# V in 4 MB transfers of all heads, P turned by VectorE, and other wo parts, in a decode kernel on one core

## The chip, the core and the metric

The kernel runs on one NeuronCore of a Trainium2 chip. TensorE (PE) multiplies, VectorE (DVE) and ScalarE (ACT) work elementwise and move PSUM to SBUF, GpSimd (POOL) prepares constants, and SyncE (SP) issues most of the DMA transfers, which sixteen DMA engines carry out. The metric is the device time of one execution in microseconds. A DMA engine moves a transfer as contiguous runs; a run is one packet in the trace's DMA packet records, and the completion of a transfer is one packet of 4 bytes on each engine.

## The reference

Four sequences (B = 4) with one token each. The token is normalized, goes through attention over a window of a cache and, beside it, through an MLP with a residual; the results are added.

```
xn  = layernorm(x)                                   # 4 x 1 x 576
A:  q = xn @ wq                                      # 32 query heads of 128, 16 K/V heads
    k, v = last 2048 of 8192 keys of the caches      # 4 x 16 x 2048 x 128 bf16 each
    p = softmax(q k^T / sqrt(128));  o = p v
    A = concat(o) @ wo                               # wo: 4096 x 576
B:  h = gelu(layernorm(xn) @ w1); hs = shifted(h) @ w2; x1 = xn + hs
    B = x1 + gelu(layernorm(x1) @ w3) @ w4           # w3: 576 x 4608, w4: 4608 x 576
out = x + A + B
```

With one token per sequence all four shifts of h give zeros, so hs is zero. What is read is 33.6 MB of K, 33.6 MB of V and some 21 MB of weights; the output is 4 x 576.

## The kernel before

The program is written by hand: each engine has a list of operations with keys (`add(engine, emit, waits, sig, key)`), the list is sorted by key, and each operation waits for the named signals of others. So the key sets the order on an engine, and on SP's queue the order in which transfers are requested. Two parts of TensorE's program are loops (K and V).

*Weights and MLP.* SP first requests wq, w1, w2, w3, w4, then K. While K's first chunks come, TensorE computes q and the whole MLP; `MO1` is the signal that w4's products are done and that the buffer `vring`, which held w3 and w4, is free. q lies in the memory of `acc` for a while.

*K stage.* K comes in 16 chunks (`CH`) of 2 MB: one sequence and four heads, every partition with 64 keys of one head, a run of 16 KB in memory (`kv_src`, partition = 32 key groups x 4 heads). `kring` has four slots; chunk c + 4 is requested when chunk c is transposed (signal `T...`). TensorE transposes K in blocks (L496), VectorE and ScalarE copy the blocks to `ktb` (L480, L479), and the scores accumulate in PSUM (L503), 128 partitions for 128 pairs of sequence and query head.

*Softmax and the turning of P.* After the last chunk VectorE takes the maximum (L509) and ScalarE the exponents in four quarters (L513). The probabilities must then stand with the keys on the partitions: VectorE multiplies each quarter with four masks (`dve_mask`, L521, 16 instructions), TensorE gathers it with 16 small matmuls per quarter (`pe_PT`, L530), ScalarE copies to SBUF (L539), TensorE permutes (L541), ScalarE copies again (L543) into `PT`.

*V stage.* V comes in 16 chunks of 2 MB like K's into `vring` (five slots, `NVS = 5`; the last chunk goes into `kring`). The first five are requested after `MO1`, behind the sixteenth K request, the others when the slot's products are done (`PV...`). For each chunk VectorE builds the padded stationary operand (L559: 512 columns, zero for the other heads), TensorE does 16 matmuls of 512 columns in four column tiles that run beside each other (`emit_PV`, L567), VectorE multiplies the 128x512 result with a mask (L585) and sums it over four (L588) into `acc`, a small matmul against a selection adds up the partitions (`emit_fold`, L573), and VectorE scales by the reciprocal sums into `OTn` (L591). Near the end ten matmuls on zeros (`pe_idle`, L578) are put in.

*wo.* The 32 rows per partition come in five parts, `WO_ROWS = (12, 10, 7, 2, 1)`, into `kring`, requested behind V's last chunk. `OTn` is transposed (L601), permuted (L602) and copied to `ORT` (L603); then each part gives two matmuls per row, one for each half of the output (`acc_mm`, L386), and the result is copied (L628, L629) and stored.

Of the kernel before, what the change touches and what calls it, by code (L numbers as in the profile page):

```python
# [12 lines left out]
NKT = 16  # L13
# [3 lines left out]
NVS = 5  # L17
ACT_EVAC = (1, 4, 7)
WO_ROWS = (12, 10, 7, 2, 1)
IDLE = {NKT - 2: 5, NKT - 1: 5}  # L20
# [14 lines left out]
def bass_parallel_sum__sliding_block_cached__mixer_s_mlp__decode_kernel(  # L35
# [23 lines left out]
    CH = [(b, gq) for gq in range(4) for b in range(B)]  # L59
    x2 = A_x.rearrange("b s d -> (b s) d")  # L60
# [3 lines left out]
    with ExitStack() as ctx:  # L64
# [12 lines left out]
        vslot = lambda c: vring[:, c % NVS * UE:(c % NVS + 1) * UE] if c < NC - 1 else kslot(0)  # L77
# [8 lines left out]
        wot = kring[:, UE:UE + 32 * D].rearrange("p (r n) -> p r n", r=32)  # L86
        assert 32 * D <= 3 * UE
# [13 lines left out]
        P4 = cut(4 * NU * 512).rearrange("p (q t u i) -> p q t u i", q=4, t=16, u=NU)  # L101
        PTx = cut(4 * 512).rearrange("p (q x) -> p q x", q=4)
        PTpad = cut(NVS * NT * 2 * NU).rearrange("p (s t u e) -> p s t u e", s=NVS, t=NT, u=NU)
        tmp = [cut(2 * 512).bitcast(FP32).rearrange("p (t d) -> p t d", t=4) for _ in range(2)]
        assert _o <= NKT * 1024
        PTv = PT_t[:].rearrange("p (t c e) -> p t c e", t=NT, c=NC)
# [18 lines left out]
        q_sb = acc[:].rearrange("p a b -> p (a b)").bitcast(BF16)[:, 0:1024].rearrange("p (k x) -> p k x", k=2)  # L125
# [5 lines left out]
        permT_bf = sb("permT_bf", [128, 128], BF16)  # L131
        ident_f = sb("ident_f", [128, 128], FP32)
        ones_f = sb("ones_f", [128, 128], FP32)
        mask4 = sb("mask4", [128, NU], FP32)
        maskd = sb("maskd", [128, 4], FP32)
        sel_f = sb("sel_f", [128, 32], FP32)
        sel_bf = sb("sel_bf", [128, 32], BF16)
        sel8 = sb("sel8", [128, 2 * NU], FP32)
        mU = sb("mU", [128, NU], FP32)
        mU_bf = sb("mU_bf", [128, NU, 2], BF16)  # L140
# [19 lines left out]
        PTps = [ps[:, 4 + k, :].rearrange("p (t x) -> p t x", t=16) for k in range(4)]  # L160
        OTps = [ps[:, 4, 8 * k:8 * k + 8] for k in range(NVS)]
        PVb = [0, 1, 2, 3, 6]
# [20 lines left out]
        for k in range(NVS):  # L183
            for nm in ("PD", "FF", "AA", "OO"):
                S[nm, k] = sem(f"{nm}{k}")
# [31 lines left out]
        for c in range(NC):  # L217
            k, i = c % NVS, c // NVS
            ev_val[f"PV{c}"] = ("PV", c + 1)
            ev_val[f"fold{c}"] = ("FO", c + 2)  # L220
            ev_val[f"pad{c}"] = (("PD", k), i + 1)
            ev_val[f"F{c}"] = (("FF", k), i + 2)
            ev_val[f"A{c}"] = (("AA", k), i + 1 + (k == NVS - 1))
            ev_val[f"O{c}"] = (("OO", k), i + 1 + (k >= NVS - 2))
# [26 lines left out]
        for nm, k in [("FF", k) for k in range(NVS)] + [("OO", NVS - 2), ("OO", NVS - 1)]:  # L251
            P(lambda e, nm=nm, k=k: e.sem_inc(S[nm, k], 1), key=-87)

# [3 lines left out]
        mask_of(mask4, "mask4", ident_f[:].rearrange("p (u x) -> p u x", u=NU))  # L257
        mask_of(maskd, "maskd", ident_f[:].rearrange("p (j t y) -> p t j y", j=4, t=4), AX.XY)
        mask_of(sel_f, "sel_f", ident_f[:].rearrange("p (u x) -> p x u", u=NU))
        mask_of(sel8, "sel8", ident_f[:].rearrange("p (k x) -> p x k", x=2 * NU))  # L260
        add("dve", lambda e: e.tensor_copy(out=sel_bf[:], in_=sel_f[:]), waits=["sel_f"], sig="sel_bf", key=-7.9)
        mask_of(mU, "mU", ident_f[:].rearrange("p (i u) -> p u i", u=NU))
        for x in range(2):
            add("dve", lambda e, x=x: e.tensor_copy(out=mU_bf[:, :, x], in_=mU[:]), waits=["mU"], sig=f"mU_bf{x}", key=-7.8)
# [16 lines left out]

        t_done = lambda c: f"T{NBLK * c + NBLK - 1}"
        ev_v = []
# [3 lines left out]
        for c in range(NC):  # L287
            w = [t_done(NC - N_CB)] if c == NC - 1 else [f"PV{c - NVS}"] if c >= NVS else ["MO1"]
            ev_v.append(add_dma([(vslot(c), kv_src(A_v_cache, c))], ("v", c % NVS if c < NC - 1 else NVS), w, KS + c))
        wos = A_wo.rearrange("(p r) n -> p r n", r=32)  # L290
        ev_wo, WOR, a = [], [], 0
        for n, rc in enumerate(WO_ROWS):
            ev_wo.append(add_dma([(wot[:, a:a + rc, :], wos[:, a:a + rc, :])], ("wo", n), [t_done(NC - 1)], KS + NC + n))
            WOR.append((a, a + rc))
            a += rc
# [221 lines left out]
        def dve_mask(q):  # L517
            def f(e):
                ins = None
                for u in range(NU):  # L520
                    ins = e.tensor_scalar(out=P4[:, q, :, u, :], in0=P_sb[:, q, :].rearrange("p (t i) -> p t i", t=16),  # L521
                                          scalar1=mask4[:, u:u + 1], scalar2=None, op0=ALU.mult)
                return ins
            return f

        def pe_PT(q):
            def f(e):
                ins = None
                for t in range(16):
                    ins = e.matmul(PTps[q][:, t, :], lhsT=P4[:, q, t].rearrange("p u i -> p (u i)"), rhs=sel_bf[:],  # L530
                                   start=True, stop=True, skip_group_check=True)
                return ins
            return f
        for q in range(4):
            k0 = KS + 0.2 + 0.1 * q
            add("dve", dve_mask(q), waits=[f"exp{q}", "mask4"], sig=f"P4_{q}", key=k0)
            add("pe2", pe_PT(q), waits=[f"P4_{q}"] + (["sel_bf"] + [f"E{NB - 1 - k}" for k in range(4)] if q == 0 else []),
                sig=f"PTp{q}", key=k0)
            add("act", lambda e, q=q: e.activation(out=PTx[:, q, :], in_=ps[:, 4 + q, :], func=ACTF.Copy),  # L539
                waits=[f"PTp{q}"], sig=f"PTx{q}", key=k0 + 0.05)  # L540
            add("pe2", lambda e, q=q: e.matmul(ps[:, q, :], lhsT=permT_bf[:], rhs=PTx[:, q, :], start=True, stop=True),  # L541
                waits=[f"PTx{q}", "permT_bf"], sig=f"PTy{q}", key=k0 + 0.11)
            add("act", lambda e, q=q: e.activation(out=PT_t[:, 512 * q:512 * (q + 1)], in_=ps[:, q, :], func=ACTF.Copy),  # L543
                waits=[f"PTy{q}"], sig=f"PT{q}", key=k0 + 0.16)
# [5 lines left out]
            waits=["diag", "ones_f", "PT3"], sig="rinvp", key=KV + 0.5)  # L550
        add("dve", lambda e: e.tensor_copy(out=rinvB[:].rearrange("p (c u e) -> p c u e", u=NU, e=2),
                                           in_=rinvps.rearrange("p (u c e) -> p c u e", u=NU, e=2)),
            waits=["rinvp"], sig="rinvB", key=KV + 1.5)


        def dve_pad(c):
            b, gq = CH[c]
            cc = 4 * b + gq
            return lambda e: e.tensor_tensor(out=PTpad[:, c % NVS],  # L559
                                             in0=PTv[:, :, cc, :].unsqueeze(2).to_broadcast([128, NT, NU, 2]),  # L560
                                             in1=mU_bf[:].unsqueeze(1).to_broadcast([128, NT, NU, 2]), op=ALU.mult)

        def emit_PV(e, k, v):
            ins = None
            for g in range(NT // 4):
                j = g % 4
                ins = e.matmul(ps[32 * j:32 * j + 32, PVb[k], :], lhsT=PTpad[:, k, 4 * g:4 * g + 4].rearrange("p t u e -> p (t u e)"),  # L567
                               rhs=v[:, 512 * g:512 * (g + 1)], start=(g < 4), stop=(g >= 12),
                               tile_position=(0, 32 * j), skip_group_check=True)
            ins.then_inc(S["PV"], 1)  # L570

        def emit_fold(e, k):
            e.matmul(OTps[k], lhsT=acc[:, k, :], rhs=sel8[:], start=True, stop=True, skip_group_check=True).then_inc(S["FO"], 1)  # L573

        def pe_idle(n):
            def f(e):
                for _ in range(n):
                    e.matmul(ps[:, 5, :], lhsT=zeros_bf[:, 0:128], rhs=zeros_bf[:, :], start=True, stop=True)  # L578
            return f
        for c in range(NC):  # L580
            b, gq = CH[c]
            k = c % NVS
            w = [f"PV{c - NVS}"] if c >= NVS else [f"PT{q}" for q in range(4)] + ["mU_bf1"]
            add("dve", dve_pad(c), waits=w, key=KV + 2 * max(c - 1, 0) + 0.2, inc=(("PD", k), 1))
            add("dve", lambda e, c=c: e.tensor_tensor(out=tmp[c % 2], in0=ps[:, PVb[c % NVS], :].rearrange("p (t d) -> p t d", t=4),  # L585
                                                      in1=maskd[:].unsqueeze(2).to_broadcast([128, 4, 128]), op=ALU.mult),
                waits=[f"PV{c}", "maskd"], key=KV + 2 * c + 0.6, inc=(("FF", k), 1))
# [28 lines left out]
        for n, (r0, r1) in enumerate(WOR):  # L616
            def f(e, r0=r0, r1=r1, hs=(0, 1)):
                ins = None
                for r in range(r0, r1):
                    for h in hs:  # L620
                        ins = acc_mm(e, h, ORT[:, r, :], wot[:, r, HALF * h:HALF * (h + 1)], stop=(r == 31))
# [112 lines left out]
```

## Time and profile before

| | |
|---|---|
| median of three runs | 215.36 us (215.35 to 215.39) |
| the profiled execution's own time, and its span | 215.12 us, 213.9 us |
| moved, and mean rate over the span | 88.64 MB, 414 GB/s |
| busy: TensorE, VectorE, ScalarE | 71%, 55%, 30% of the span |
| mean granted TensorE clock | 0.832 of full speed |
| K stage, V stage, wo (last landing of K 122.2; first V product 140.4; ORT ready 205.6) | 49 to 129 us, 140 to 204 us, 206 to 212 us |

The page cuts the span into 40 slices of 5.35 us: a row of tenths for each engine, the clock, the DMA share and GB/s. Its queue table gives packets, bytes and the share of the sixteen engines' time. A table by stretches gives for each stretch the busy time of PE, PE's weight loads, DVE, ACT and POOL with the number of instructions, then the clock, the DMA share and GB/s. The chain of waits is followed back from the last instruction; each piece has its start, its length and what it was.

### The profile page before, as it was taken

Reading aid. Unit: us, or ns where it says so; the run is one execution under the profiler, and the core shown is the slowest. Engines: PE = TensorE matmul, PEld = TensorE weight load, DVE = VectorE, ACT = ScalarE, POOL = GpSimd, SP = SyncE. Lnnn points to the kernel's source line nnn. Section 1 sums busy time; section 2 is a strip of 40 time slices with the busy share of each in tenths; the row PEclk is TensorE's granted clock in tenths of the full one; section 3 lists DMA queues with packets and bytes.
Section 4 is the critical chain, followed back from the end, with each engine's and each line's share of the span. In section 5 each row is a group of like instructions: output and inputs, shape, how many; then the busy total and the mean of one; then the engine's idle time right before and its main releaser. Section 6 shows DMA issues by size and latency. Waiting matters only on the chain.

```text
span 213.9 us, 4528 instructions
## 1 busy us (share of the span) xinstructions
PE 151.6 (71%) x1984; PEld 96.9 (45%) x1987; DVE 116.8 (55%) x240; ACT 64.3 (30%) x78; POOL 12.7 (6%) x20
## 2 busy tenths in 40 slices
PE   2038478578999999999999971788444455555964
PEld 0013126337878877888887860434111122212332
DVE  4962720015767776667677666759934333334520
ACT  2001032003666666556666665810000000000000
POOL 8950000000000000000000000000000000000000
PEclk9999958889999999999999999557855555555699
DMA  7999989999999999999999999999999999999993
GB/s 277 411 385 494 427 376 440 429 417 420 435 429 420 423 438 426 423 426 438 427 420 429 435 426 420 434 429 417 429 435 423 426 432 435 423 426 432 426 400 122
DMA packets 6802, 88.64 MB, mean 414 GB/s; under 512 B 764, under 2 KB 1160, under 8 KB 1928
## 3 DMA queue, kind: packets, MB, share of 16 engines
q1 hardware_dynamic: 6776, 88.50, 97.7%
q8 instruction: 7, 0.11, 0.2%
q14 instruction: 3, 0.02, 0.0%
q10 hardware_dynamic: 16, 0.01, 0.0%
HBM read 88.49 MB, written 0.00 MB: 414 GB/s over the span
## 4 chain that ended last, share of the span: by engine, by line
DMA 68%; PE 17%; DVE 9%; ACT 3%; issue 1%; SPq 1%
DMA kring<-in_A_k_cache_dram 41%; DMA kring<-in_A_wo_dram 16%; DMA vring<-in_A_v_cache_dram 10%; PE ps L496 7%; DVE xn_bf L312 4%; PE ps L567 3%; PE ps L503 2%; PE ps L358 2%; SPq L202 1%; DVE rmax L509 1%; DVE ktb L521 1%; ACT ktb L539 1%; ACT PT L543 1%; DMA x_sb<-in_A_x_dram 1%; PE ps L386 1%
## 5 line engine op out<-in xcount | busy, mean ns | idle before, releaser
L480 DVE COPY ktb<-ps 128x1024 bf16<-128x1024 bf16 x80 | 53.8, 690 | 24.7 <-PE ps L496 24.2
L496 PE MATMUL ps<-perm_bf,kring 128*128 128x128 bf16 x1024 | 62.6, 219 | 3.0 <-DMA kring<-in_A_k_cache_dram 2.1
L496 PEld LDWEIGHTS ps<-perm_bf,kring 128*128 128x128 bf16 x1024 | 57.2, 98 | 12.6 <-issue 9.8
L479 ACT ACTIVATE ktb<-ps 128x1024 bf16<-128x1024 bf16 x48 | 49.2, 1024 | 31.6 <-PE ps L496 30.8
L567 PE MATMUL ps<-vring,ktb 128*32 128x512 bf16 x240 | 25.8, 575 | 23.2 <-DMA vring<-in_A_v_cache_dram 23.2
L585 DVE TENSOR_TENSOR ktb<-ps,maskd 128x512 f32<-128x512 f32 x16 | 11.0, 690 | 29.6 <-PE ps L567 29.5
L629 ACT ACTIVATE out_sb<-ps 4x288 bf16<-4x288 f32 x1 | 0.4, 402 | 72.4 <-PE ps L386 72.4
L567 PEld LDWEIGHTS ps<-vring,ktb 128*32 128x32 bf16 x240 | 7.1, 121 | 30.9 <-issue 27.3
L503 PE MATMUL ps<-ktb,Qs 128*32 128x512 bf16 x272 | 17.8, 382 | 1.2 <-ACT ktb L479 1.2
L588 DVE TENSOR_REDUCE acc<-ktb 128x128 f32<-128x512 f32 x16 | 16.4, 1028 | 0.5
L573 PEld LDWEIGHTS ps<-sel,acc 128*128 128x128 f32 x34 | 7.3, 268 | 14.6 <-issue 8.8
L573 PE MATMUL ps<-sel,acc 128*128 128x8 f32 x34 | 8.8, 331 | 2.5 <-DVE OTn L591 2.5
L503 PEld LDWEIGHTS ps<-ktb,Qs 128*32 128x32 bf16 x272 | 5.8, 95 | 6.7 <-DVE ktb L480 1.4
L322 PE MATMUL ps<-ident_bf,xn_bf 4*128 4x4 bf16 x8 | 0.6, 170 | 11.4 <-DVE xnT L339 8.9
L386 PE MATMUL ps<-vring,h2T_sb 128*4 128x288 bf16 x72 | 6.4, 348 | 2.5 <-DMA vring<-in_B_w_dram 2.5
L559 DVE TENSOR_TENSOR ktb<-PT,mU_bf 128x512 bf16<-128x512 bf16 x16 | 6.6, 416 | 2.1 <-ACT PT L543 2.1
L312 DVE TENSOR_SCALAR xn_bf<-xn_bf,mv,rstd 4x576 bf16<-4x576 bf16 x1 | 7.4, 7430 | 0.0
L245 POOL MEMSET ktb<- 128x8192 bf16 x1 | 6.9, 6925 | 0.0
L530 PE MATMUL ps<-sel_bf,ktb 128*128 128x32 bf16 x64 | 2.4, 189 | 5.5 <-DVE ktb L521 5.5
L386 PE MATMUL ps<-kring,ORT 128*4 128x288 bf16 x64 | 4.4, 286 | 2.4 <-DMA kring<-in_A_wo_dram 1.8
L322 PEld LDWEIGHTS ps<-ident_bf,xn_bf 4*128 4x128 bf16 x8 | 0.4, 112 | 12.3 <-DVE ragsrc L315 9.0
L386 PEld LDWEIGHTS ps<-vring,h2T_sb 128*4 128x4 bf16 x72 | 3.6, 100 | 5.1 <-DMA vring<-in_B_w_dram 2.7
(117 smaller groups left out, 96.4 us busy)
## 6 DMA issues: line engine op xcount, KB each, us to landing
kring<-in_A_k_cache_dram SPq DMA_DIRECT2D x16, 2048.0 KB, 14.7
vring<-in_A_v_cache_dram SPq DMA_DIRECT2D x15, 2048.0 KB, 22.4
vring<-in_B_w_dram SPq DMA_DIRECT2D x1, 4608.0 KB, 24.9
kring<-in_A_wq_dram SPq DMA_DIRECT2D x1, 4096.0 KB, 12.4
vring<-in_B_w_dram SPq DMA_DIRECT2D x1, 3456.0 KB, 34.7
kring<-in_A_v_cache_dram SPq DMA_DIRECT2D x1, 2048.0 KB, 26.7
ktb<-in_B_w_dram SPq DMA_DIRECT2D x3, 576.0 KB, 14.5
vring<-in_B_w_dram SPq DMA_DIRECT2D x1, 1728.0 KB, 38.3
```

What stands on the lines that cost most here:

```text
L245: P(lambda e: e.memset(ktb[:, NKT // 2 * 1024:NKT * 1024], 0.0), key=-92, inc=(("E", LB - 2), 1))
L312: add("dve", lambda e: e.tensor_scalar(out=dst[:], in0=src[:], scalar1=mv[:, idx, 0:1], scalar2=rstd[:, idx:idx + 1], op0=ALU.subtract, op ...
L386: return e.matmul(ACC[h], lhsT=lhsT, rhs=rhs, start=start, stop=stop, tile_position=(0, 32 * h), skip_group_check=True)
L479: return "act", lambda e: e.activation(out=ktbuf[:, n % NKT], in_=tb[n % 4], func=ACTF.Copy)
L480: return "dve", lambda e: e.tensor_copy(out=ktbuf[:, n % NKT], in_=tb[n % 4])
L496: ins = e.transpose(tb[j % 4][:, t, :], kslot_t(k)[:, 8 * kb + t, :], perm_bf[:])
L503: ins = e.matmul(Sps[32 * u:32 * u + 32, q, :].rearrange("p (t i) -> p t i", t=16), lhsT=Qs[:, k, 32 * u:32 * u + 32], rhs=ktgrp[:, (4 * k ...
L559: return lambda e: e.tensor_tensor(out=PTpad[:, c % NVS], in0=PTv[:, :, cc, :].unsqueeze(2).to_broadcast([128, NT, NU, 2]), in1=mU_bf[:].u ...
L567: ins = e.matmul(ps[32 * j:32 * j + 32, PVb[k], :], lhsT=PTpad[:, k, 4 * g:4 * g + 4].rearrange("p t u e -> p (t u e)"), rhs=v[:, 512 * g: ...
L573: e.matmul(OTps[k], lhsT=acc[:, k, :], rhs=sel8[:], start=True, stop=True, skip_group_check=True).then_inc(S["FO"], 1)
L585: add("dve", lambda e, c=c: e.tensor_tensor(out=tmp[c % 2], in0=ps[:, PVb[c % NVS], :].rearrange("p (t d) -> p t d", t=4), in1=maskd[:].un ...
L588: add("dve", lambda e, c=c: e.tensor_reduce(out=acc[:, c % NVS, :], in_=tmp[c % 2].rearrange("p t d -> p d t"), axis=AX.X, op=ALU.add), wa ...
```

## The change

- *V's transfers.* Eight chunks (`VCH`) of 4 MB, each all 16 heads of a sequence and half of its 2048 keys. A partition holds 128 keys of one head, a run of 32 KB (`v_src`, partition = 16 heads x 8 key groups). Four slots (`NVS = 4`): two in `vring`, two in `kring`. Chunks 0 and 1 are requested after `MO1`, 2 and 3 when K's chunks 13 and 15 are transposed, the others when the products of the chunk four before are done. The last chunk comes in two transfers of 96 and 32 keys per partition (`VCUT`).
- *The products.* 64 matmuls of 256 columns per chunk in two column tiles of 64. The pad is 4096 columns, with two buffers instead of five. The result is 128x256 and is masked and added in two VectorE operations on 128x128. One fold per chunk with a 128x32 selection; two folds accumulate, and `OTn` is written once per sequence. Zero matmuls: eight after the third and five after the fourth chunk of each of the loop's two turns.
- *P.* VectorE transposes each quarter in 32x32 blocks; four groups of four matmuls against a picking matrix (`pick_bf`, made by GpSimd) follow when all four quarters are there, and ScalarE (one of them VectorE) copies to `PT`. The masks, the permuting matmuls and a copy per quarter are gone.
- *wo.* Parts of 14, 9, 5, 3 and 1 rows, all in `vring`: the first part's place is free from the start and its request has no wait of its own, the others wait for V's chunk 4.
- *Two small things.* SP requests 25 elements of wo into an unused buffer between the first two parts, and GpSimd three times 17 runs of 64 bytes after the scores of K's chunk 6. q lies in `vring` instead of `acc`.

```diff
-NVS = 5
+NVS = 4
-WO_ROWS = (12, 10, 7, 2, 1)
-IDLE = {NKT - 2: 5, NKT - 1: 5}
+WO_ROWS = (14, 9, 5, 3, 1)
+VCUT = 96
+IDLE = {2: 8, 3: 5}
...
+    VCH = [(b, hf) for b in range(B) for hf in range(2)]
+    NCV, NTV = len(VCH), 2 * NT
+    VPART = [[(0, NTV)]] * (NVS - 1) + [[(0, VCUT), (VCUT, NTV)]]
...
-        vslot = lambda c: vring[:, c % NVS * UE:(c % NVS + 1) * UE] if c < NC - 1 else kslot(0)
+        vslot = lambda k: (vring, vring, kring, kring)[k][:, k % 2 * 2 * UE:(k % 2 + 1) * 2 * UE]
...
+        def v_src(c, u0, u1):
+            b, hf = VCH[c]
+            k0 = Sk - W + hf * (W // 2)
+            return A_v_cache[b, :, k0:k0 + W // 2, :].rearrange("h (i t) d -> h i (t d)", t=NTV)[:, :, Dh * u0:Dh * u1]
...
-        for c in range(NC):
-            w = [t_done(NC - N_CB)] if c == NC - 1 else [f"PV{c - NVS}"] if c >= NVS else ["MO1"]
-            ev_v.append(add_dma([(vslot(c), kv_src(A_v_cache, c))], ("v", c % NVS if c < NC - 1 else NVS), w, KS + c))
+        for c in range(NCV):
+            w = [f"PV{c - NVS}"] if c >= NVS else [t_done(NC - N_CB + 2 * c - 3)] if c >= 2 else ["MO1"]
+            for n, (u0, u1) in enumerate(VPART[c % NVS] if c >= NVS else [(0, NTV)]):
+                add_dma([(vslot(c % NVS)[:, Dh * u0:Dh * u1], v_src(c, u0, u1))], ("v", c % NVS, n), w, KS + c + 0.1 * n)
+        ev_mark = add_dma([(h2_sb[0:1, 0, 0:25], A_wo[0:1, 0:25])], "mark", (), KS + NC + 0.5)
+        ev_mk = add_dma([(h2_sb[0:17, 1, 32 * n:32 * n + 32], A_wo[0:17, 0:32]) for n in range(3)], "mark2", ["SC6"], 0, engine="pool")
...
-            ev_wo.append(add_dma([(wot[:, a:a + rc, :], wos[:, a:a + rc, :])], ("wo", n), [t_done(NC - 1)], KS + NC + n))
+            ev_wo.append(add_dma([(wot(a, rc), wos[:, a:a + rc, :])], ("wo", n), [f"PV{NCV - NVS}"] if n else [], KS + NC + n))
...
+        def pe_PT(hi):
+            def f(e):
+                ins = None
+                for g in range(4):
+                    ins = e.matmul(ps[32 * g:32 * g + 32, 4 + hi, :].rearrange("p (t b e) -> p t b e", b=B, e=2),
+                                   lhsT=pick_bf[:, hi, :], rhs=PTx_v[:, :, :, g, :], start=True, stop=True,
+                                   tile_position=(0, 32 * g), skip_group_check=True)
+                return ins
+            return f
         for q in range(4):
+            add("dve", lambda e, q=q: e.transpose(PTx[:, q, :], P_sb[:, q, :]), waits=[f"exp{q}"], sig=f"PTx{q}", key=KS + 0.2 + 0.1 * q)
...
+        def emit_PV(e, k, u0, u1):
+            ins = None
+            for g in range(u0 // 2, u1 // 2):
+                j = g % 2
+                ins = e.matmul(ps[64 * j:64 * j + 64, k, 0:256], lhsT=PTpad[:, k % 2, 2 * g:2 * g + 2].rearrange("p t h e -> p (t h e)"),
+                               rhs=vslot(k)[:, 256 * g:256 * (g + 1)], start=(g < 2), stop=(g >= NTV // 2 - 2),
+                               tile_position=(0, 64 * j), skip_group_check=True)
+            return ins
...
+        with nc.Fori(0, NCV // NVS, engines=[PE]) as it:
...
             for k in range(NVS):
                 e.wait_ge(S["PD", k], turn)
+                e.wait_ge(S["AA", k], turn)
+                for n, (u0, u1) in enumerate(VPART[k]):
+                    e.wait_ge(S["v", k, n], landed)
+                    ins = emit_PV(e, k, u0, u1)
+                ins.then_inc(S["PV"], 1)
+                e.wait_ge(S["AA", (k - 1) % NVS], after if k else turn)
+                if k % 2 == 1:
+                    e.wait_ge(S["OO", k // 2], turn)
                 emit_fold(e, (k - 1) % NVS)
+                for _ in range(IDLE.get(k, 0)):
+                    e.matmul(ps[:, 6, :], lhsT=zeros_bf[:, 0:128], rhs=zeros_bf[:, :], start=True, stop=True)
```

## The prediction

> **What bounds the kernel now.** I read the page's table of slices first, then its queue table, then rates by stretch, then the chain of waits, then the last fifteen microseconds in order of time.
>
> ```profile
> DMA  7999989999999999999999999999999999999993
> GB/s 277 411 385 494 427 376 440 429 417 420 435 429 420 423 438 426 423 426 438 427 420 429 435 426 420 434 429 417 429 435 423 426 432 435 423 426 432 426 400 122
> q1 hardware_dynamic: 6776, 88.50, 97.7%
> q8 instruction: 7, 0.11, 0.2%
> ```
> The sixteen DMA engines are full from the first slice to the last but one. All 88.5 MB go through one queue, which is busy 97.7% of the span, so no wait of an engine in the middle costs anything until it lets this stream run dry.
>
> ```profile
> 6.20:11.00 4.80, 0.00 (x0) 0.00 (x0) 4.76 (x2) 0.00 (x0) 4.80 (x2) 1.00 1.01 437
> 61.00:122.20 61.20, 60.12 (x1000) 49.02 (x997) 43.16 (x75) 37.89 (x37) 0.00 (x0) 1.00 1.01 428
> 156.60:195.80 39.20, 19.44 (x148) 8.25 (x152) 16.91 (x32) 0.00 (x0) 0.00 (x0) 0.50 1.01 429
> ```
> The last column is GB/s. K (second row) and V (third), both in 16 KB runs, move at 428 and 429; the first row is wq, in 32 KB runs, at 437. The third row also shows TensorE at clock 0.50 and busy only half the time in the V stage: it waits for data.
>
> ```profile
> 171.30 1.92 PE ps L567 x16
> ...
> 175.56 34.97 DMA kring<-in_A_wo_dram
> 210.54 0.04 issue
> 210.58 1.44 PE ps L386 x20
> 212.01 0.44 DVE out_sb L628
> ```
> The chain ends in wo: a landing at 210.54, which is that of the 7-row part, then 20 matmuls without a gap (7, 2 and 1 rows, two each), the copy and the store. So the end is that of the stream plus a short tail.
>
> From the trace's DMA packet records come three more numbers. A 2 MB K or V transfer takes each engine 4.894 us (eight runs, 611 ns from start to start, and a completion of 6 ns); wq's 32 KB runs follow each other in 1209.4 ns once started, w3's 36 KB runs in 1363. The sixteen engines do equal work but end their last row between 209.05 and 211.22 us: a code load (the 7 packets on q8, 16 KB each) costs the engine that carries it its own 1.06 us and 0.47 us on the next packet, about 1.55 us, and the seven fell on seven different engines. The end is that of the last engine.
>
> **The change part by part.** The profiled execution took 215.12 us (span 213.9); the median of the runs is 215.36, 0.24 above. I sum differences and apply them to the median.
>
> *V as eight 4 MB transfers in 32 KB runs.* Per 4 MB: now 2 x 4.894 = 9.788 us; in 32 KB runs 8 x 1.2094 + 0.006 = 9.681. By w3's runs scaled by bytes (1363 x 32/36 = 1211.5) it is 9.698. Eight times 0.107 or 0.090 is -0.86 or -0.72: I take **-0.80 us**. What the trace doesn't show is sixteen engines reading many heads at once: each run now belongs to one of 16 heads that lie 2 MB apart, where before the engines read neighbouring 16 KB pieces of four heads in turn. Bounds: by the 437 against 428 GB/s of the stretches, 33.6 MB would gain 1.6 us; wq's second and third rounds, when all engines had just started together, took about 1238 ns, 28 more than its settled runs, and at that 64 runs per engine lose 64 x (1238 - 1223) = 1.0 us. I stay at the settled rows, because the engines are up to 2.1 us apart by then and not in step.
>
> [...] The row first: K and V of before read four heads 2 MB apart one after the other and lose nothing (428 GB/s). [...]
>
> *Buffers.* Now V0 to V4 (five slots) are asked for behind K15, and V5 needs the products of V0, which end at 142.38; the queue would run dry at 122.2 + 5 x 4.89 = 146.7, so 4.3 us are in hand. After: V0 and V1 behind K15, V2 and V3 when K's transposes of chunks 13 and 15 are done (the last at about 127.1), all before V1 lands at 122.2 + 2 x 9.68 = 141.6; V4 needs the products of V0 and the queue is fed until 160.9. **0 us.**
>
> *P turned by VectorE.* Removed: 16 mask products (L521, 348 ns), 64 + 4 matmuls, 8 ACT copies of 0.6 us. Added: four VectorE transposes of 128x512; the one of 128x128 (L601) took 311 ns, so at most 4 x 1.25 = 5.0 us after the first exponent (132.7) gives 137.7; then 16 matmuls in four groups (0.6 us by L541) and four copies (0.6 to 0.69): 139 us. The pad is eight times as large: 8 x 0.416 = 3.3 us at most, so the first product starts near 142.3 instead of 140.44. It needs V0 (131.9), and hides behind the stream: the V4 request comes near 150, 11 us before the queue is dry. **0 us**; a cost would start only beyond those 11 us.
>
> *Two column tiles.* The work per 4 MB goes from 32 matmuls in eight rounds of 512 columns (2 x 1.90 us at clock 0.5, 2 x 1.05 at 1.0) to 64 in 32 rounds of 256, twice the columns: 7.6 us at clock 0.5, 4.2 at 1.0. A chunk takes 9.68 us to come. VectorE per chunk: pad 3.3, two small products of about 0.3 each (L551 moved 128x128 from PSUM in 0.28) against twice 0.69 + 1.03 now. Both fit: **0 us** before the last chunk.
>
> *The last chunk and the wo parts.* Before: the last engine's completion is at 211.21, seen 0.43 later as for the 7-row part (210.11, matmuls at 210.58), so the last row is there at 211.64 and the matmuls end at 211.98, 0.34 behind it, because 20 queue up behind 7 rows. After, by the same packet records, parts of 9, 5, 3 and 1 rows take 3.1, 1.77, 1.08 and 0.40 us, so the 5-row part lands 1.5 us before the last; 16 matmuls at 70 ns are 1.1 us, and only the last two remain, 0.15 us: **-0.19 us**. That needs the earlier work done: V7's second part, a quarter of it, lands 11.1 us before the end, near 199.8; idle matmuls and the first part of V7 keep TensorE busy until then, at clock 1.0 (it rose at 201.2 before with 10 idle matmuls; now 13 and denser products). Products to 202.7, fold, five idle, fold: 204.6; the turn to ORT took 1.3 (204.31 to 205.62 now): 205.9; 46 matmuls for 14 and 9 rows: 209.1, when the 5 rows land at about 209.4. Cover 0.3 us; beyond it every us late is one us on the end.
>
> *Code.* TensorE executed 3971 instructions; less three repeats of the K loop (640 each) and two of the V loop (180) it stores about 1690, and loaded 7 packets. The new V loop has about 554 instead of 180, the P stage 104 fewer, the tail 56 fewer: about 1900, one packet more. On an engine with 0.7 us or less of lateness it adds at most 0.15 to the end, on one of the seven late ones up to 1.55. I take **+0.10**.
>
> *Marks.* POOL issues three transfers of 17 runs of 64 B after the scores of chunk 6, SP one of 50 B between the wo parts (0.5 us of its time, nothing urgent behind: the other wo requests go out at about 176). A 576 B packet took 29 ns, a 4 B one 9, so 17 runs cost 0.15 to 0.5 us if one engine takes them all; nothing if the engine isn't among the late ones, 1.5 us if all three meet the last engine. Nine of sixteen engines have over 1.4 us in hand: **+0.15**. POOL's two selects and a memset at the start stand beside 40 us of queued weights: 0.
>
> *Sum:* -0.80 - 0.19 + 0.10 + 0.15 = -0.74: 215.36 - 0.74 = **214.6 us**.
>
> **The rivals.**
> *The heads collide* (slower): V's 32 KB runs from heads 2 MB apart slow each other. For it: wq's first runs, all engines in step, took 1.24 to 2.10 us instead of 1.21. Against it: the engines are spread by 2.1 us in the V stage. It decides from a run of 1222 ns on (64 runs x 11.6 ns eat the 0.74), and shows as slower from 1229; at 1238, the row above, +1.0 instead of -0.8 gives 216.4; at 1260, 3% over two runs of 16 KB, 217.8.
> *A late engine gets more* (between same and slower): the extra code load or the marks fall on one of the four engines within 0.35 us of the last. For it: seven of sixteen are already late; against: the seven loads met seven different engines. 0.5 to 1.5 us instead of 0.25: 214.9 to 215.9.
> *TensorE is late at the end* (slower): the clock is still 0.5 when V7 comes. V7 takes 7.6 instead of 4.2 us, the folds and idle matmuls double: ORT near 210.5 and 64 matmuls after it, 4.5 us: about 218.5. Against it: TensorE is busy almost without a gap from V6's landing (190).
> *More is gained*: runs at 437 GB/s, or a narrower spread of the engines: -1.6 - 0.19 and nothing lost, 213.6.
>
> **How the numbers follow.** Forecast (214.0 to 215.0) 0.50; late engine 0.17; heads collide 0.17; TensorE late 0.06; more gained 0.10. A difference of 0.2% (0.43 us) is about what can be told from none. Faster: 0.48 of the forecast and 0.10: 0.58; same: 0.02 and 0.10 of the late engine: 0.12; slower: the rest, 0.30. The range leaves out the better half of "more gained", the worse half of the collisions and the late TensorE: 213.8 to 216.5; the forecast's own is 214.0 to 215.0.
>
> **What would show it.** V stage at about 433 GB/s, V landings 9.68 us apart and all DMA slices full: the first step. Two matmuls after the last landing, at 70 ns: the wo step. Eight or nine packets on q8; the pool's queue beside it. The prediction is wrong if the V stage falls below 428 GB/s, if a slice in the V stage drops under 9, or if the chain's last part starts at ORT instead of at a wo landing.

## The result and the profile after

The changed kernel took 295.4 us (median of six runs, 288.11 to 298.19) against 215.36 us for the kernel before beside it (215.20 to 216.40). Of the changed kernel's runs two are in the faster of two states (288.11 and 291.69 us), and the ratio of 1.3453, with a 95% interval of 1.3344 to 1.3562, is theirs. The forecast was 214.6 us and a little faster. The profiled execution of the changed kernel took 288.11 us, its span 286.9 us.

The same rows of the page's slices (one slice is now 7.17 us) and of its queue table as were shown of before, for the changed kernel:

```profile
DMA  7999999999999999999999999999999999999993
GB/s 293 409 465 390 450 416 432 423 420 427 427 436 416 432 431 418 402 203 215 210 219 218 224 238 233 210 244 228 219 219 219 233 242 219 223 223 235 256 410 132
q1 hardware_dynamic: 5770, 88.49, 97.9%
q8 instruction: 8, 0.13, 0.2%
```

The DMA row says that nothing is wrong: nines from end to end, and the queue is busy 97.9% of a span that is 73 us longer. The row below it says the opposite. From slice 17 on (122 us, where V begins) the same busy engines move 203 to 256 GB/s instead of 430, and with wo, in slice 38, the rate is back at 410. A busy share counts the time that packets are under way, and here it is as full at either rate: 1.00 at 225 GB/s in this V stage (below), 1.00 at 431 in that of the 32-head kernel of the experiments.

The table by stretches (the last three columns are the granted TensorE clock, the DMA share and GB/s) of the changed kernel, K's stage and then V's:

```profile
61.00:122.00 61.00, 60.13 (x1002) 48.87 (x995) 42.77 (x75) 37.68 (x38) 1.69 (x3) 1.00 1.02 422
140.00:260.00 120.00, 46.06 (x475) 38.99 (x474) 23.11 (x25) 1.68 (x3) 0.00 (x0) 0.66 1.00 225
```

V is 33.6 MB: 78 us at 430 GB/s, 149 us at 225, so 71 of the 73 us are there. Its 32 KB packets, whose median is 1216 ns in the good case (below), had a median of 2485 ns. The chain of waits of the changed kernel (start, length, what), a part of the V stage and the end:

```profile
145.29 5.35 PE ps L575 x64
150.64 0.34 PE ps L581 x2
150.98 12.32 another core or an unknown queue
163.30 0.14 issue
163.44 5.18 PE ps L575 x64
168.62 0.34 PE ps L581 x2
168.96 12.66 another core or an unknown queue
...
284.22 0.70 PE ps L401 x8
284.92 0.44 DVE out_sb L627
```

The chain has no name for what it waited for, some 12 us before each chunk. The groups of instructions have one; the last part of the row is the idle time before the group and what ended it:

```profile
L575 PE MATMUL ps<-kring,ktb 128*64 128x256 bf16 x256 | 22.3, 354 | 41.6 <-DMA kring<-in_A_v_cache_dram 41.6
```

TensorE waits for V to land. Neither it nor VectorE has become the bound (busy 46.06 and 23.11 of those 120 us). By the packet records the last packet of wo ends at 284.12 us, so the last product (284.92) comes 0.80 us behind it, as long a tail as before. So all but some 2 us of the loss is the rate of V's transfers. What makes it slow is the question of the experiments.

### The profile page after: what moved, and what is told of

Same layout as the page of the kernel before. It is cut to its first block, busy times and chain, and to the rows that moved or that the text cites. A ratio compares the mean times of both kernels' runs of the same rounds, so it can differ in the third digit from the quotient of the medians.

```text
span 286.9 us, 4856 instructions
## 1 busy us (share of the span) xinstructions
PE 168.5 (59%) x2186; PEld 125.9 (44%) x2191; DVE 104.8 (37%) x190; ACT 61.8 (22%) x73; POOL 15.4 (5%) x26
## 3 DMA queue, kind: packets, MB, share of 16 engines
q1 hardware_dynamic: 5770, 88.49, 97.9%
## 4 chain that ended last, share of the span: by engine, by line
DMA 32%; PE 31%; another core or an unknown queue 27%; DVE 7%; issue 1%; ACT 1%; SPq 0%; DVEq 0%
DMA kring<-in_A_k_cache_dram 32%; PE ps L575 16%; PE ps L511 6%; DVE xn_bf L327 3%; PE ps L401 2%; PE ps L518 2%; PE ps L709 2%; PE ps L373 2%; PE ps L581 1%; DVE ktb L544 1%; DVE rmax L524 1%; DVE ktb L568 1%; PE ps L538 1%; DMA x_sb<-in_A_x_dram 1%
## 5 line engine op out<-in xcount | busy, mean ns | idle before, releaser
L575 PE MATMUL ps<-kring,ktb 128*64 128x256 bf16 x256 | 22.3, 354 | 41.6 <-DMA kring<-in_A_v_cache_dram 41.6
L575 PE MATMUL ps<-vring,ktb 128*64 128x256 bf16 x256 | 22.8, 362 | 38.5 <-DMA vring<-in_A_v_cache_dram 35.8
L589 DVE TENSOR_SCALAR ktb<-ps,maskd 128x128 f32<-128x128 f32 x8 | 2.8, 351 | 108.8 <-PE ps L575 108.8
L575 PEld LDWEIGHTS ps<-kring,ktb 128*64 128x64 bf16 x256 | 20.7, 147 | 43.3 <-issue 42.6
L575 PEld LDWEIGHTS ps<-vring,ktb 128*64 128x64 bf16 x256 | 20.3, 151 | 41.0 <-issue 24.4
L518 PE MATMUL ps<-ktb,Qs 128*32 128x512 bf16 x272 | 18.6, 396 | 1.2 <-ACT ktb L494 1.2
L568 DVE TENSOR_TENSOR ktb<-PT,mH_bf 128x4096 bf16<-128x4096 bf16 x8 | 18.2, 2282 | 0.0
L401 PE MATMUL ps<-vring,ORT 128*4 128x288 bf16 x64 | 5.9, 344 | 1.8 <-DMA vring<-in_A_wo_dram 1.8
L538 PE MATMUL ps<-ktb,pick_bf 128*32 128x512 bf16 x16 | 2.0, 631 | 6.4 <-DVE rinv L556 6.4
L709 PE MATMUL ps<-zeros_bf 128*128 128x512 bf16 x22 | 5.4, 379 | 0.2
```

The lines of the kernel that those rows point to most:

```text
L401: return e.matmul(ACC[h], lhsT=lhsT, rhs=rhs, start=start, stop=stop, tile_position=(0, 32 * h), skip_group_check=True)
L518: ins = e.matmul(Sps[32 * u:32 * u + 32, q, :].rearrange("p (t i) -> p t i", t=16), lhsT=Qs[:, k, 32 * u:32 * u + 32], rhs=ktgrp[:, (4 * k ...
L538: ins = e.matmul(ps[32 * g:32 * g + 32, 4 + hi, :].rearrange("p (t b e) -> p t b e", b=B, e=2), lhsT=pick_bf[:, hi, :], rhs=PTx_v[:, :, :, ...
L568: return lambda e: e.tensor_tensor(out=PTpad[:, c % 2], in0=PTv[:, hf, :, b, :].unsqueeze(2).to_broadcast([128, NTV, Hkv, 2]), in1=mH_bf[: ...
L575: ins = e.matmul(ps[64 * j:64 * j + 64, k, 0:256], lhsT=PTpad[:, k % 2, 2 * g:2 * g + 2].rearrange("p t h e -> p (t h e)"), rhs=vslot(k)[: ...
L709: e.matmul(ps[:, 6, :], lhsT=zeros_bf[:, 0:128], rhs=zeros_bf[:, :], start=True, stop=True)
```

## The experiments

Theory at the start: "the heads collide", as the rival in the prediction had it, because the sixteen engines read heads 2 MB apart. In all diffs `k0` is the first key and `h`, `i`, `t` are head, group of keys, key. Kernels without an interval were run once; the changed kernel's own six runs spread over 10 us, so differences of a few us among kernels near 290 us say nothing. Most of these kernels read other data than the computation needs and only time a pattern.

**Other distances between the heads.** If addresses 2 MB apart are the trouble, other distances cure it. These kernels read heads' windows 2 MB less 4 KB, less 256 B, less 128 KB, and 1 MB and 512 KB apart, by a view of the cache with a shorter head; the first one:

```diff
-            k0 = Sk - W + hf * (W // 2)
-            return A_v_cache[b, :, k0:k0 + W // 2, :].rearrange("h (i t) d -> h i (t d)", t=NTV)[:, :, Dh * u0:Dh * u1]
+            k0 = Sk - W + hf * (W // 2) - 256
+            s_ = Sk - 16
+            flat = A_v_cache[b].rearrange("h s d -> (h s) d")[0:Hkv * s_, :].rearrange("(h s) d -> h s d", s=s_)
+            return flat[:, k0:k0 + W // 2, :].rearrange("h (i t) d -> h i (t d)", t=NTV)[:, :, Dh * u0:Dh * u1]
```

> The changed kernel, but each head's V window is read 16 keys (4 KB) earlier than the last head's, so neighbouring heads' reads lie 2 MB less 4 KB apart instead of 2 MB; transfers, runs, buffers and products stay as they are (other keys of V are read, so the output is another). Theory 'pitch' (the sixteen engines read sixteen heads in step, a power of two apart, and meet in the same part of HBM): the 32 KB packets fall from about 2400 to about 1210 ns and the time to 214 to 216 us. Rival 'long runs' (32 KB runs or 4 MB transfers are slow by themselves once the buffers alternate): nothing changes, 285 to 298 us. Rival 'engines' (VectorE or TensorE holds the stream back): nothing changes either.

> As the 4 KB case, but only one key (256 B) less per head, 3.8 KB over all sixteen. Theory 'pitch' with pieces of HBM of some KB: the reads still meet, more than 260 us. If any distance that is not exactly a power of two is enough: 214 to 216 us.

> The changed kernel with each head's window 512 keys (128 KB) earlier than the last head's, so that sixteen heads read at sixteen places of the 2 MB (other keys are read, so the output is another). If heads collide in pieces of HBM larger than the 60 KB that the 4 KB case spread them over: 214 to 220 us. If the distance doesn't matter: 285 us or more.

Measured: 287.83, 293.55 and 290.55 us. For 1 MB:

> The same at 1 MB, a chunk in 16 MB, eight regions of 2 MB. Theory 'places': slower than 512 KB and faster than 2 MB, 220 to 285 us. Theory 'gaps': 285 us or more. If only the full power of two of 2 MB hurts: 214 to 217 us.

Measured: 289.04 us, and for 512 KB, where the theory "places" (many distant regions read at once halve the rate) expected 214 to 217 us, 292.88. Five distances, five times the same loss: the distance in memory is not the cause.

**Shorter runs, fewer heads, no marks.** V's chunks in two transfers with 16 KB runs (`VPART = [[(0, NT), (NT, NTV)]] * NVS`); chunks of 8 heads and all their keys, with the key group outermost; and the change without the two small transfers. The source pattern of the 8 heads (the picking matrix, pads and folds follow it and are left out here):

```diff
-            return A_v_cache[b, :, k0:k0 + W // 2, :].rearrange("h (i t) d -> h i (t d)", t=NTV)[:, :, Dh * u0:Dh * u1]
+            return A_v_cache[b, 8 * hf:8 * hf + 8, Sk - W:Sk, :].rearrange("h (i t) d -> i h (t d)", t=NTV)[:, :, Dh * u0:Dh * u1]
```

> The changed kernel, but every V chunk comes in two transfers of 64 keys per partition, so in 16 KB runs of the length used before; heads, partitions and distances stay. Theory 'pitch': 16 KB packets near 1200 instead of 611 ns and 285 to 300 us. Rival 'long runs': back to 215 to 217 us.

> V still in eight 4 MB transfers of 32 KB runs, but a chunk is eight heads with all 2048 keys and the key group is the outer index (16 groups of 128 keys), so the sixteen engines read neighbouring 32 KB pieces of one head at a time and go through the heads in turn, as in the kernel before; the picking matrix, pads, masks and folds follow, in four column tiles of 32. Theory 'pitch': 32 KB packets at about 1210 ns, and with them the sum of the prediction, 214 to 215.3 us. Rival 'long runs': above 280 us.

> The changed kernel without the small transfers of SP and GpSimd. Theory 'where it reads': no difference, 285 to 298 us. Rival 'marks' (the GpSimd queue, once used, halves the engines' rate): 214 to 216 us.

Measured: 280.19, 293.15 and 290.94 us. With 16 KB runs a packet takes a median of 1126 ns against 613 before, and the table by stretches has 244 GB/s from 140 to 260 us where the changed kernel has 225. That is a little better and still far from 430: the length of a run isn't it. Eight heads are no better than sixteen, and the marks have no part in it.

**The same chunk from one place.** Each chunk is one contiguous piece of 4 MB, the transfers, slots and products unchanged.

```diff
-            k0 = Sk - W + hf * (W // 2)
-            return A_v_cache[b, :, k0:k0 + W // 2, :].rearrange("h (i t) d -> h i (t d)", t=NTV)[:, :, Dh * u0:Dh * u1]
+            k0 = 0
+            flat = A_v_cache[b].rearrange("h s d -> (h s) d")[4 * hf * Sk:4 * hf * Sk + Hkv * 1024, :].rearrange("(h s) d -> h s d", s=1024)
+            return flat[:, k0:k0 + W // 2, :].rearrange("h (i t) d -> h i (t d)", t=NTV)[:, :, Dh * u0:Dh * u1]
```

> The changed kernel, but each V chunk is one contiguous piece of 4 MB (other keys and heads are read, so the output is another): 32 KB runs one after the other as wq has them; transfers, buffers, order and marks as in the changed kernel. Theory 'where it reads' (the slow half is a matter of the addresses that are read at the same time): about 1210 ns per packet and 214 to 216 us. Rival 'how it is issued' (buffers, marks, two transfers in flight, the V stage's other work): stays at 285 us or more.

Measured: 214.70 us, the V stage at 430 GB/s. So 32 KB runs into the same buffers, with the same code around them, lose nothing. At this point "many distant places at once" looked proved, and it was wrong. Eight heads read from one contiguous 4 MB, in the order of the eight-head kernel above (16 key groups outermost, 8 heads inside), spoke against it:

> The kernel with eight heads per chunk and the key group outermost, but its eight pieces of 512 KB lie one behind the other in 4 MB (other data are read). Every engine still jumps from piece to piece after each 32 KB run. Theory 'places': fast, 214 to 216 us. Theory 'jumps' (long runs with jumps between them are slow): 285 us or more.

Measured: 293.33 us. One place, and slow.

**The kernel before with other heads.** Its V chunks of four heads were taken four apart (`gq:Hkv:4`, so 8 MB between heads), and then as eight heads by half the keys, in 16 KB runs of the same 2 MB transfers (the diff is the second one's):

```diff
+        def v_src(c):
+            b, gq = CH[c]
+            k0 = Sk - W + gq % 2 * (W // 2)
+            h0 = 8 * (gq // 2)
+            return A_v_cache[b, h0:h0 + 8, k0:k0 + W // 2, :].rearrange("g (i t) d -> i g (t d)", t=NT)
...
-            ev_v.append(add_dma([(vslot(c), kv_src(A_v_cache, c))], ("v", c % NVS if c < NC - 1 else NVS), w, KS + c))
+            ev_v.append(add_dma([(vslot(c), v_src(c))], ("v", c % NVS if c < NC - 1 else NVS), w, KS + c))
```

> The kernel before, with only this changed: a V chunk has the heads g, g+4, g+8, g+12 (8 MB apart) instead of four neighbours (2 MB apart); the products then meet other heads, so the output is another. If heads collide by address bits above 4 MB: slower than 216 us, up to 300. If not: 215.4.

> The kernel before, with only V's chunk changed: eight heads by 1024 keys instead of four by 2048, still 2 MB, 16 KB runs and the key group outermost (the products meet other keys, so the output is another). Theory 'places': slow, above 250 us, although nothing of the changed kernel is in it. If the long runs or 4 MB transfers are needed for the loss: 215.4 us.

Measured: 215.09 us and 291.49 us. The second one is the kernel before in everything but the source pattern of V, and it falls to the rate of the changed kernel. Its slices and queue:

```profile
DMA  7999999999999999999999999999999999999994
GB/s 290 409 460 394 439 435 429 420 418 427 431 429 434 429 423 422 346 221 215 218 215 217 219 219 217 221 217 226 219 228 217 221 217 219 219 217 219 218 394 191
q1 hardware_dynamic: 6776, 88.50, 98.5%
```

Nothing in the new V stage is needed for the loss. In the kernel's text the source pattern of a transfer is a nest of counts: an outermost one, and inside each of its steps a number of runs. Every chunk here has 128 runs, one per partition. What all slow kernels have in common is the outermost count of this pattern: 16 (with 8 runs inside). Before has 32 key groups outermost with 4 heads inside. The contiguous chunk, whose 16 x 8 runs follow each other without a gap, can be written as one row of 128. No trace shows the form in which a pattern reaches the engines.

**A gap of 2 KB.** The theory 'split' of the expectations below is this: a chunk with 16 outermost comes at half the rate, one with 32 or 128 does not. If so, the contiguous chunk must become slow, 285 to 295 us, as soon as its 128 runs can't be written as one row. A gap of 2 KB after each eight runs does that and leaves the addresses all but the same:

```diff
-...[4 * hf * Sk:4 * hf * Sk + Hkv * 1024, :].rearrange("(h s) d -> h s d", s=1024)
+...[4 * hf * Sk:4 * hf * Sk + Hkv * 1032, :].rearrange("(h s) d -> h s d", s=1032)
```

> The contiguous case (214.7 us) with one size changed: the sixteen pieces of 256 KB are 258 KB apart, a gap of 2 KB after each, so that a chunk can no longer be told as 128 runs in a row but only as 16 times 8 (other data are read). [...] Any theory on addresses in HBM: 214 to 216 us, since what is read is nearly the same.

Measured: 293.10 us. Two kilobytes cost 78 us. The slices of the contiguous chunk:

```profile
DMA  7999989999999999999999999999999999999993
GB/s 265 424 380 501 428 376 428 428 427 418 433 424 427 424 430 427 430 427 430 425 427 427 461 418 436 442 413 445 424 421 442 418 448 430 424 421 408 434 408 120
```

The slices of the one with the gap, where the rate falls in slice 16 and is halved from slice 17 on:

```profile
DMA  7999999999999999999999999999999999999980
GB/s 293 407 453 416 442 411 427 424 424 427 429 431 423 431 426 431 319 216 216 216 219 220 220 243 238 227 220 220 222 238 229 216 216 225 225 226 225 287 345 32
```

**32 outermost.** The opposite test: more distant heads, but 32 of them outermost. A chunk is the 32 heads of two sequences by a quarter of the keys, still 128 runs of 32 KB in 4 MB, and the rest is the changed kernel; beside it the same without the marks, and the kernel before with the new wo parts alone.

```diff
-            b, hf = VCH[c]
-            k0 = Sk - W + hf * (W // 2)
-            return A_v_cache[b, :, k0:k0 + W // 2, :].rearrange("h (i t) d -> h i (t d)", t=NTV)[:, :, Dh * u0:Dh * u1]
+            p, Q = c // 4, c % 4
+            k0 = Sk - W + Q * (W // 4)
+            return A_v_cache[2 * p:2 * p + 2, :, k0:k0 + W // 4, :].rearrange("b h (i t) d -> (b h) i (t d)", t=NTV)[:, :, Dh * u0:Dh * u1]
```

> The changed kernel with V's chunk taken as 32 heads (all heads of two sequences, 2 MB apart) by a quarter of the keys, four runs of 32 KB per head: outermost count 32, still 4 MB, 32 KB runs and distant heads (the products meet other heads and keys, so the output is another). Theory 'split': full rate, about 1212 ns per packet, and the sum of the prediction, 214.6 us (214.0 to 215.0). Theories on addresses: 32 distant places at once must be as slow as 16, 285 us or more.

> The same without the small transfers of SP and GpSimd, to measure the term of +0.15 us: if 'split' holds, 214.45 us, between 213.9 and 214.6; if the marks fall on engines that end early, no difference.

> The kernel before with only the wo parts changed to 14, 9, 5, 3 and 1 rows, to measure the term of -0.19 us: 215.2 us. If the last rows weren't on the path: 215.36.

Measured, against 215.41 us of before in that comparison: 214.87 us (ratio 0.9977, 0.9967 to 0.9987), 214.76 us (0.9970, 0.9960 to 0.9980) and 215.18 us (0.9993, 0.9984 to 1.0002). Thirty-two heads, each 2 MB from the next, come at 431 GB/s. The V stage in the table by stretches of the first of the three:

```profile
160.00:195.00 35.00, 21.65 (x255) 19.88 (x257) 8.80 (x10) 0.00 (x0) 0.00 (x0) 0.76 1.00 431
```

Its queue table:

```profile
q1 hardware_dynamic: 5770, 88.49, 97.6%
q8 instruction: 8, 0.13, 0.2%
```

The decisive numbers side by side (packets of V's transfers in the V stage, from the DMA packet records):

```
source of a chunk                     outermost   run     quartiles of a packet, ns   us of that run
before, 4 heads                       32          16 KB    612 /  613 /  618        215.12
before, 8 heads x half the keys       16          16 KB   1169 / 1201 / 1239        291.49
the change, 16 heads                  16          32 KB   2234 / 2485 / 2518        288.11
8 heads contiguous, groups outermost  16          32 KB   2276 / 2467 / 2520        293.33
16 x 8 runs, contiguous               128 in row  32 KB   1213 / 1216 / 1220        214.70
the same with gaps of 2 KB            16          32 KB   2229 / 2465 / 2518        293.10
32 heads of two sequences             32          32 KB   1213 / 1216 / 1220        214.80
```

With 128 runs in every chunk, 16 outermost and eight inside are one and the same; no run here tells them apart, and no other count was tried.

**The whole computation with 32 outermost.** The two 32-head kernels put the keys of V where P doesn't have them, so they only time the change. Two more carry it through: P's picking matrix, pad and products for two sequences by a quarter of the keys (a pad of 64 columns for each key of a partition, 128 matmuls of 128 columns per chunk, one fold per pair of sequences), without the marks. In the first all chunks came in two or three parts; in the second six of eight came whole, and ten matmuls on zeros stand between the permutation of `OTn` and the first part of wo. The second against the first:

```diff
-    VPART = [[(0, NT), (NT, NTV)]] * (NVS - 1) + [[(0, NT), (NT, 112), (112, NTV)]]
+    VPART = [[(0, NTV)]] * (NVS - 1) + [[(0, NT), (NT, 112), (112, NTV)]]
...
+            for _ in range(N_KEEP):
+                ins = e.matmul(ps[:, 2, :], lhsT=zeros_bf[:, 0:128], rhs=zeros_bf[:, :], start=True, stop=True)
```

> The whole computation with V's chunk as in e13 (all 32 heads of two sequences by a quarter of the keys, outermost count 32, 32 KB runs): the picking matrices, pads (8192 columns per chunk) and products follow; 128 matmuls of 128 columns per chunk in two column tiles, accumulated over four chunks, one fold per two sequences, V's chunks in two parts (the last of each four in three), two zero matmuls, no marks. Theory 'split': the stream runs at full rate as in e13, and the end depends on TensorE, at 60 ns per matmul 7.7 us per 9.7 us chunk: 214.6 us, between 214.2 and 215.6. If TensorE needs more than 76 ns per matmul it becomes the bound of the V stage: 216 to 225 us.

> The whole computation with V as chunks of two sequences and a quarter of the keys (32 heads outermost), as in e16_two_sequences, with two changes: six of the eight chunks come whole again, in 32 KB runs (only the fourth of each turn is split, in 64, 48 and 16 keys per partition), and ten matmuls on zeros follow the permutation of OTn, so that TensorE isn't idle for the 2.4 us before the first part of wo. Theory (the loss of e16 was two things: 16 KB runs in the stream, and a granted clock that fell in the idle gap and made the 64 wo matmuls 109 ns each): the V stage at 430 GB/s or more, wo matmuls at 67 to 70 ns, only the last ones behind the last landing: 214.8 us (214.4 to 215.2), against 215.3 of before. Rival (the clock falls whatever TensorE does there, or the larger chunks come too late for it): wo matmuls again at about 109 ns, 216 us or more.

Measured: 216.58 us (1.0054, 1.0034 to 1.0073) and 216.04 us (1.0034, 1.0022 to 1.0045), both above what was expected. The profiled execution of the first took 217.08 us, the longest of its seven. The wo products of the first in order of time (in brackets the idle time ahead of them and what ended it):

```profile
206.97 6.96 PE L392 MATMUL ps<-vring,ORT 128*4 128x288 bf16 x64 [2.41 <-DMA vring<-in_A_wo_dram]
```

The same view of the second has them in four pieces, of which this is the first:

```profile
206.44 1.88 PE L393 MATMUL ps<-vring,ORT 128*4 128x288 bf16 x28 [0.21 <-DMA vring<-in_A_wo_dram]
```

The chain of the first ends so:

```profile
206.93 0.04 issue
206.97 7.01 PE ps L392 x63
213.98 0.43 DVE out_sb L613
```

And that of the second:

```profile
178.74 33.55 DMA vring<-in_A_wo_dram
212.28 0.04 issue
212.33 0.70 PE ps L393 x8
213.03 0.43 DVE out_sb L621
```

In the first, TensorE stood idle for 2.41 us before the first part of wo, and the 64 products took 6.96 us, 109 ns each; its chain ends in them. In the second it ran the first 28 in 1.88 us (67 ns), the granted clock from 207 us on was 1.00 instead of 0.63, and the chain ends with a landing again. That is what the theory on the clock expected, though V's parts changed in the same edit, so the zero matmuls weren't tried alone.

The clock was the smaller part of the loss. By the packet records the last wo packet ends at 212.77 us in the first and 212.23 in the second, against 210.82 in the 32-head kernel without marks: the stream itself is late in both, by 1.95 and 1.41 us. With the tail of 0.80 us that the second has behind its last packet, the first would have ended its products at 213.57 instead of 213.98, so the slow clock cost some 0.4 us of that execution.

Part of that is the packets' own time: summed over the queue it is 209.28 us per engine in the first and 208.74 in the second, against 208.28, so 1.00 and 0.46 us more. The other 0.95 us, in both, isn't settled; it is how far apart the engines end. In the second kernel nine or ten packets are under way at a time from 209.25 to 210.25 us and two from 211.0 to 212.0, against 16 at 656 of 740 points between 20 and 205 us in the kernel before. So two of sixteen engines work alone for over 1 us. The queue table of both kernels has more code loads:

```profile
q8 instruction: 10, 0.16, 0.3%
```

In the second, five of the ten fall after 140 us, against three of eight in the kernel without marks. The engines stop in steps of about 1.5 us, which is the cost of one load by the prediction's row (1.06 us and 0.47 us). That the last two engines carried two loads each fits this, but the packet records don't name the engine, so it is an inference, not shown. No version here that computes everything beats the kernel before.

## Why the prediction was wrong

*What bounds the kernel.* Right: the stream sets the end, before and after. But one sign that the prediction named for its first step, full DMA slices, can't tell full rate from half: in the changed kernel every slice of the V stage is full at 225 GB/s. Its other sign, a V stage below 428 GB/s, did tell.

*V in 32 KB runs, -0.80 us: this step failed.* As written it took the length of a run from wq's settled packets (1209 ns) and asked only what the engines read: sixteen heads 2 MB apart. The doubt was put in memory addresses, and its bounds came from wq's packets when all engines had just started (1238 ns), 28 ns more than the settled ones. Measured were 2485 ns and +73 us in the profiled execution. Length and distance are both innocent: the median is 1216 ns with 32 heads 2 MB apart. What was not looked at is the shape of the source pattern. wq, w3 and K, whose rows the price came from, were all 32 or 128 outermost; the change made it 16, and no row of the profile before had that. The term itself was well sized where the shape allows it: with 32 outermost the time of the queue's packets per engine falls from 209.02 us to 208.39, and 208.28 without the marks, 0.63 and 0.74 against 0.80.

*The rival "the heads collide"* named the right transfers and the right sign, by a wrong mechanism, and its worst price (217.8, so 2.4 us) was thirty times too small. The runs show no cost of the distance: 431 GB/s with heads 2 MB apart, and half the rate (224 GB/s) where the groups of runs lie 258 KB apart.

*Why 16 is slow* was not shown, only that it is: in the V stage 219 to 244 GB/s with 16 outermost, 427 to 431 with 32 and 430 with one row of 128. No run here shows which engine carries a packet or which partitions it fills.

*Buffers, P and column tiles, 0 us each: right*, read in the 32-head kernel. P's four transposes took 2.72 us (bound 5.0), the pad 2.28 on average (bound 3.3), the first product began at 141.20 (forecast 142.3), the 64 products of V7 took 3.69 us, 58 ns each (forecast 4.2), and the stream never paused (DMA share 1.01 from 122 to 141 us, 1.00 from 160 to 195). The rows, from that kernel's instructions in order of time:

```profile
132.72 2.72 DVE L545 STREAM_TRANSPOSE ktb<-Qpad 128x512 bf16<-128x512 bf16 x4 [0.85 <-ACT Qpad L529]
141.20 3.68 PE L576 MATMUL ps<-vring,ktb 128*64 128x256 bf16 x64 [2.67 <-DVE ktb L569]
197.88 3.69 PE L576 MATMUL ps<-kring,ktb 128*64 128x256 bf16 x64
205.04 1.88 PE L402 MATMUL ps<-vring,ORT 128*4 128x288 bf16 x28 [1.06 <-DMA vring<-in_A_wo_dram]
```

The last row is the end's cover: the first wo products wait 1.06 us for their data, so ORT (204.46) was in time, as forecast for 205.9.

*The wo parts, -0.19 us: not confirmed.* Alone, in the kernel before, they gave -0.23 us, in an interval that holds no change. The chain of that kernel ends so:

```profile
175.95 35.25 DMA kring<-in_A_wo_dram
211.20 0.04 issue
211.24 0.70 PE ps L386 x8
211.94 0.44 DVE out_sb L628
```

Eight products, not two, follow the last wait that the chain shows, since the parts of 3 rows and of 1 row land almost together: the term counted only the last part's two products. From the last packet's end to the last product are 211.94 - 211.09 = 0.85 us, against 212.02 - 211.22 = 0.80 before: the tail is as long as it was.

*Code, +0.10, and marks, +0.15.* One code load more came (8 on q8), as forecast; what it cost by itself no run shows. With and without marks differ by 0.11 us, less than the two intervals can separate. The reading that seven of sixteen engines were late is one short: in the kernel before eight or nine packets are under way from 210.0 to 210.75 us, so eight engines are still at work.

*The sum, where the shape allows it,* is near: -0.54 us measured with 32 outermost, marks and all, against -0.74.

*"TensorE is late at the end"*, priced for a clock of 0.5 when V7 comes, was no part of the loss. In the changed kernel V7's first 48 products did take 4.33 us (90 ns each, against 58 ns in the 32-head kernel), but the chain still ends with a landing and eight products (0.70 us). In the first of the two full kernels the slow clock came later, in the wo products, and that is another path than the one that was priced.

## What to carry to other kernels

Read a DMA stage by GB/s and by the time of a packet, never by the busy share alone: here it was 1.00 at 225 GB/s and 1.00 at 431. When a transfer into 128 partitions is rearranged, count its outermost dimension: in this case 32 or 128 kept about 430 GB/s and 16 gave 219 to 244, whatever the run length, the transfer size or the addresses. The price that was taken from a transfer of another shape, 1209 ns, met 2485; if no row of the profile has the new shape, the range has to say so.

## What the runs showed that was not expected

- Sixteen outermost (eight runs inside) halved the rate of V's transfers, 219 GB/s against 428 or 429: 291.49 us against 215.21 in the kernel before beside it, by V's source pattern alone, and a 2 KB gap that takes the one-row form from a contiguous chunk costs 78 us (214.70 to 293.10).
- The distance between heads, from 512 KB to 2 MB and off by 256 B, 4 KB or 128 KB, changes nothing that can be seen: 287.8 to 293.6 us with 16 outermost.
- After 2.4 us without work on TensorE its last 64 products took 109 ns each; in a kernel with ten matmuls on zeros in the gap, and other parts of V, the first 28 took 67. The execution lost only some 0.4 us by it, because the stream ended late in both.
